# A recurrent-attention and mixture-of-experts kernel: two more blocks of the first expert ahead of the recurrence's end, conversions behind evictions, w2 after the tokens

## The chip, the cores and the metric

One core of one Trainium2 chip runs the whole kernel. The metric is the device time of one execution in microseconds (us). The engines are TensorE (PE, with its weight loads PEld), VectorE (DVE), ScalarE (ACT), GpSimd (POOL) and SyncE (SP), which here only issues DMAs.

## The reference

Two stages follow each other. The first is a linear recurrence over 768 steps for 4 x 8 heads of width 40; the second sends each of the 3072 rows to one of 8 experts.

```python
for t in range(S):                       # S = 768, state is [B, H, 40, 40]
    y[:, :, t] = einsum('bhd,bhde->bhe', rt, state)
    Sa = einsum('bhde,bhe->bhd', state, at)
    state = state * wt[:, :, None, :] - einsum('bhd,bhe->bhde', Sa, bt)
    state = state + einsum('bhd,bhe->bhde', vt, kt)
x = y.transpose(0, 2, 1, 3).reshape(3072, 320)

logits = x @ w_gate                      # 8 experts
e_idx = argmax(logits, axis=1)
gate_w = softmax(logits)[e_idx]
eom = sigmoid(x @ w_output_gate)
for e in range(8):                       # w1: 320 x 1024, w2: 1024 x 320
    h = maximum(x[e_idx == e] @ w1[e], 0)
    out[e_idx == e] = gate_w * eom[:, e] * (h @ w2[e])
```

## The kernel before

**The recurrence.** Time is cut into 12 chunks (c) of 64 steps. The heads of a chunk form two groups, q = 0 and 1; (11,1) is the last group of the recurrence. For each group `crit` carries the state on, and `tail` forms the output: transposes (ptS, ptU), products pM, a mask M on DVE, the sums pY on PE, and x = pY times the decays on DVE. `route` then works on x: it writes x to DRAM (xd), transposes it on PE (pxt from ident and x), copies the result to xT on ACT, and multiplies it by the gate weights (pxt from G and xT).

**The router.** `pick` runs four times, the last time for chunk 11. On DVE it finds the best expert of each row (a one-hot table in mem), PE counts rows with matmuls on two constant matrices (tri, one), and DVE turns the counts into a slot number si. POOL then scatters records into a table in DRAM (tab). `slots` reads the table back (tr), and DVE makes tb and ti of it: for each slot of each expert the row and its weight. An expert has 480 slots in 4 tiles of 120.

**Tokens.** `tokens` has POOL gather rows of xd by ti into xg (one indirect DMA a tile), transposes them on PE in three pieces k (px), and splits each into a rounded part xh (ACT) and a remainder xl (DVE); the third piece has two more copies on ACT. A product is the sum of three rounded products (high x high, high x low, low x high).

**Weights.** `weights` loads w1 in three pieces and w2 in three (st, by SP), casts each to its high part on ACT (w1h, w2h) and subtracts on DVE for the low part (w1l, w2l). Two sets of weight buffers are used in turn, and four staging buffers st.

**An expert.** `expert` has 8 blocks. In each, eight matmuls fill a PSUM tile ph; ACT evicts it as hh = relu, and DVE as hl, the remainder. In the experts' stage there are three buffers for ph. Then for each tile of tokens 24 matmuls (three for each block) fill po, DVE scales it to y, and POOL scatters y to the output. The first two experts are done in halves of two tiles (240 slots), because half of the table is known after chunk 7; experts 2 to 7 are done whole (480 slots).

**What is early.** `early` runs as background work inside the recurrence: it converts the first expert's weights, gathers the tokens of its first half, and computes the first E0 = 4 of its 8 blocks. There ph is a tile of the recurrence's PSUM pool (px_ and a number in the rows of the order). The other blocks run in `experts`, where `unit` steps through the blocks and tiles of one expert and lets a second generator, `prep`, go one step for each: next weights and next tokens.

**What sets the order.** The code gives dependencies and priorities, and a scheduler sets the order on each engine. Each engine then works through its own order and waits where data are not there. `issue_after` adds an order between two instructions. Before the change `s.last`, the end of the last pick, is what the conversions of the second expert's weights (st1) come after.

Of the kernel before, what the change touches and what calls it, by code (L numbers as in the profile page):

```python
# [9 lines left out]
F32 = mybir.dt.float32  # L10
# [4 lines left out]
AF = mybir.ActivationFunctionType  # L15
ALU = mybir.AluOpType
# [38 lines left out]
class Att:  # L55
# [441 lines left out]
    def run(s, sink, first, then, last):  # L497

        n = s.nch
        done = object()  # L500
        batches = [[c] for c in range(FAST)] + [list(range(c, min(c + 2, n))) for c in range(FAST, n, 2)]
        ready = {}

        def preps(b):
            for c in b:
                yield from s.prep(c)
                if c + 1 < n:
                    s.scan(c + 1)
                if c == 0:
                    with s.tc.issue_after(s.mark[1]):  # L510
                        s.later()

        def inv(b):
            yield from s.tinv(b)
            for c in b:
                ready[c] = True

        def background():
            s.warm(s.ident, 40)
            s.scan(0)  # L520
            for b in batches:
                yield from preps(b)
                if b == batches[0]:
                    first()
                yield from inv(b)
            s.pre.close()
            s.idle = True
            if then:
                yield from then()
        bg = background()  # L530
        npc = 0

        def adv(k):
            for _ in range(k):
                next(bg, done)

        def need(c):
            while c not in ready:
                next(bg)
        need(0)  # L540
        with s.tc.issue_after(s.mark[1]):
            s.load_r(0, 0)
            s.load_x(0, 0)
            s.load_x(0, 1)
        tail = iter(())

        def later(k):
            while k and s.post:
                if next(s.post[0], done) is done:
                    s.post.pop(0)  # L550
                else:
                    k -= 1
        for c in range(n):
            need(min(c + 1, n - 1))
            for q in range(2):
                for i, _ in enumerate(s.crit(c, q)):
                    next(tail, None)
                    if i == 3:
                        with s.tc.issue_after(s.mark['am', 1]):
                            if q == 0:  # L560
                                s.load_r(c, 1)
                            elif c + 1 < n:
                                s.load_r(c + 1, 0)
                            if c + 1 < n:
                                s.load_x(c + 1, q)
                    adv(RATE)
                    later(1)
                while next(tail, done) is not done:
                    pass
                tail = s.tail(c, q, sink)  # L570
        last()
        for _ in tail:
            pass
        later(-1)
        for _ in bg:
            pass


E, CAP, DM, FF, NTOK = 8, 480, 320, 1024, 3072
TS = CAP // 4  # L580
E0 = 4


class Moe:
# [48 lines left out]
                s.nc.sync.dma_start(out=s.G[d:128, k, 8 * j:8 * j + 8], in_=x[r:r + 128 - d])  # L633
        s.nc.sync.dma_start(out=s.tab.rearrange("(p n) f -> p n f", p=128), in_=s.t0)

    HALF, HT, half = 7, 2, False
    NB = {3: (0, 4), 7: (4, 4), 10: (8, 3), 11: (11, 1)}

    def route(s, c, q, x, pool, psx):

        nc = s.nc
        xf = x.rearrange("p h e -> p (h e)")
        nc.sync.dma_start(out=s.xd[256 * c + 128 * q:256 * c + 128 * q + 128], in_=xf)
        pt = psx()
        for k, o in enumerate((0, 128, 192)):
            nc.tensor.transpose(out=pt[:, k], in_=xf[:, o:o + 128], identity=s.ident)
        xT = pool.tile([128, 3, 128], F32, name="xT", tag="xT", bufs=1)
        nc.scalar.copy(out=xT, in_=pt[:, 0:3])
        for k in range(3):
            nc.tensor.matmul(pt[:, 3], xT[:, k], s.G[:, k], start=(k == 0), stop=(k == 2))  # L650
        nc.scalar.copy(out=s.LG[:, 2 * c + q], in_=pt[:, 3, 0:16])
        yield
        if q and c in s.NB:
            yield from s.pick(*s.NB[c], pool, psx().rearrange("p k t -> p (k t)"))
            if c == s.HALF:

                nc.vector.tensor_tensor(out=s.base, in0=s.base, in1=s.bnd, op=ALU.max)
                s.half = True

    def pick(s, c0, n, pool, fl):  # L660
# [31 lines left out]
        V.tensor_tensor(out=sv, in0=pr, in1=ro(s.base), op=ALU.add)  # L692
        pe = fl[:, 224:232]
        for i in range(n):
            nc.tensor.matmul(pe, s.one, oh[:, i], start=(i == 0), stop=(i == n - 1))
        V.tensor_tensor(out=s.base, in0=s.base, in1=pe, op=ALU.add)
        yield
        ov = wv
# [61 lines left out]
    def weights(s, e, wp, sp, lag=0, mark=None, st=()):  # L760
# [21 lines left out]
        if not lag:  # L782
            for k in range(6):
                with ExitStack() as order:
                    for m in s.last if st else ():
                        order.enter_context(s.tc.issue_after(m))
                    halve(k, st[k] if k < len(st) else load(k))
                yield
            return
# [41 lines left out]
    def expert(s, nt, W, T, pool, ps1, ps2):  # L831
# [5 lines left out]
        for f in range(8):  # L837
            fs = slice(128 * f, 128 * f + 128)
            ph = ps1()[:, 0:TS * nt]
            seq = []  # L840
            for k in range(2):
                seq += [(w1h[:, k, fs], xh[:, k]), (w1h[:, k, fs], xl[:, k]), (w1l[:, k, fs], xh[:, k])]
            seq += [(w1h[:, 2, fs], xh[:, 2]), (w1h[:, 2, fs], xl[:, 2])]
            for i, (l, r) in enumerate(seq):
                nc.tensor.matmul(ph, l, r, start=(i == 0), stop=(i == 7))  # L845
            p, w = pool()
            a = p.tile([128, w], F32R, name="hh", tag="hh")[:, 0:TS * nt]
            b = p.tile([128, w], F32R, name="hl", tag="hl")[:, 0:TS * nt]
            nc.scalar.activation(out=a, in_=ph, func=AF.Relu)  # L849
            nc.vector.scalar_tensor_tensor(out=b, in0=ph, scalar=0.0, in1=a.bitcast(F32), op0=ALU.max, op1=ALU.subtract)  # L850
            hh.append(a)
            hl.append(b)
            yield
# [24 lines left out]
    def early(s, ctx, psx, mark):  # L878
# [21 lines left out]
        s.hp0 = ExitStack()  # L900
        hp = s.hp0.enter_context(s.tc.tile_pool(name="hp0", bufs=E0, side="right"))
        s.hp = hp, TS * 2
        s.E0 = s.expert(2, s.W0, T, lambda: s.hp, lambda: s.ps1(), lambda: s.ps2())
        s.ps1 = lambda: psx(CAP)
        for _ in range(E0):
            next(s.E0)
            yield

    def experts(s, ctx, verdict):
        tc = s.tc  # L910
# [29 lines left out]
        tabs = s.slots(tp)  # L940
        t2 = tok(tabs, 0, 2, 2)
        unit(0, 0, 2, chain(t, w))
        s.hp0.close()
        t3 = tok(tabs, 1, 2, 2)
        unit(1, 0, 2, t2)
# [4 lines left out]
        for e in range(2, E):  # L950
            n = e + 1 < E
            t = tok(tabs, e + 1, 0, 4) if n else iter(())
            with ExitStack() as order:
                if not n:
                    order.enter_context(tc.manual_schedule(engines={mybir.EngineType.PE}))
                unit(e, 0, 4, chain(wts(e + 1), t) if n else t)


class General:
# [174 lines left out]
```

## Time and profile before

| | us |
|---|---|
| median of 3 runs | 692.04 |
| lowest and highest | 689.71 to 692.27 |
| profiled execution | 689.8 |
| span of its trace (first to last instruction) | 688.0 |
| mean granted clock of TensorE | 0.966 |

The span is cut into instructions of each engine. A row of the timeline has the start, the time, the engine, the line, the operation with its tiles, and in brackets the idle time ahead of it and what ended it. Matmuls overlap, so what one costs in a sequence is the distance between starts, not its own time. A granted clock of 1.00 is 2.4 GHz, one of 0.50 is 1.2 GHz.

### The profile page before, as it was taken

Reading aid. Unit: us, or ns where it says so; the run is one execution under the profiler, and the core shown is the slowest. Engines: PE = TensorE matmul, PEld = TensorE weight load, DVE = VectorE, ACT = ScalarE, POOL = GpSimd, SP = SyncE. Lnnn points to the kernel's source line nnn. Section 1 sums busy time; section 2 is a strip of 40 time slices with the busy share of each in tenths; the row PEclk is TensorE's granted clock in tenths of the full one; section 3 lists DMA queues with packets and bytes.
Section 4 is the critical chain, followed back from the end, with each engine's and each line's share of the span. In section 5 each row is a group of like instructions: output and inputs, shape, how many; then the busy total and the mean of one; then the engine's idle time right before and its main releaser. Section 6 shows DMA issues by size and latency. Waiting matters only on the chain.

```text
span 688.0 us, 21149 instructions
## 1 busy us (share of the span) xinstructions
PE 636.0 (92%) x8871; PEld 567.0 (82%) x8871; DVE 464.1 (67%) x911; ACT 339.7 (49%) x783; POOL 237.3 (34%) x337
## 2 busy tenths in 40 slices
PE   7687988898999999989999799799999999999995
PEld 6466877787888888888888798799999998898985
DVE  8868689969986995998499544453774455554230
ACT  2577752874477367537733434433562344333120
POOL 9665321341333458214223201445242152412112
PEclk9667999999999999999999899899999999999999
DMA  6995763376356537633225722352674343521001
GB/s 139 175 190 129 177 154 68 91 174 161 99 144 168 118 86 192 164 87 113 64 78 170 209 83 81 98 159 80 200 219 117 112 135 110 190 79 33 19 11 32
DMA packets 56305, 84.45 MB, mean 123 GB/s; under 512 B 26848, under 2 KB 43515, under 8 KB 54763
## 3 DMA queue, kind: packets, MB, share of 16 engines
q1 hardware_dynamic: 52331, 74.05, 41.5%
q0 software_dynamic: 3872, 8.97, 4.5%
q8 instruction: 72, 1.18, 0.7%
q14 instruction: 30, 0.25, 0.1%
HBM read 67.59 MB, written 8.96 MB: 111 GB/s over the span
## 4 chain that ended last, share of the span: by engine, by line
PE 55%; DVE 24%; ACT 8%; DMA 7%; issue 5%; SPq 1%; POOLq 0%; POOL 0%; ACTq 0%; DVEq 0%
PE ph L845 12%; PE pa L392 5%; PE po L860 4%; PE pM L464 4%; PE po L858 4%; PE po L859 4%; DVE tmpf L314 4%; PE pl L225 4%; PE pt L163 3%; ACT N L236 3%; DVE I L116 2%; PE pS L430 2%; DVE P L116 2%; DMA out_dram<-y,ti 2%; DMA st<-in_w_dram 2%
## 5 line engine op out<-in xcount | busy, mean ns | idle before, releaser
L850 DVE SCALAR_TENSOR_TENSOR hl<-ph,hh 128x480 fp32r<-128x480 f32 (+1 forms) x76 | 41.9, 562 | 62.3 <-ACT hh L849 58.2
L863 POOL DMA_INDIRECT out_dram<-y,ti x32 | 35.3, 1104 | 137.1 <-DVE y L862 73.6
L845 PE MATMUL ph<-xh,w1h 128*128 128x480 f32 (+1 forms) x228 | 79.7, 352 | 1.7 <-DVE hl L850 1.3
L849 ACT ACTIVATE hh<-ph 128x480 fp32r<-128x480 f32 (+1 forms) x76 | 37.0, 498 | 89.5 <-PE ph L845 84.9
L858 PE MATMUL po<-w2h,hh 128*120 128x320 f32 x256 | 78.9, 312 | 0.9 <-ACT hh L849 0.9
L845 PE MATMUL ph<-xl,w1h 128*128 128x480 f32 (+1 forms) x228 | 78.4, 346 | 0.0
L859 PE MATMUL po<-w2l,hh 128*120 128x320 f32 x256 | 77.9, 308 | 0.0
L860 PE MATMUL po<-w2h,hl 128*120 128x320 f32 x256 | 76.2, 310 | 0.0
L240 POOL TENSOR_SCALAR_AFFINE_SELECT LA<-LA 64x192 f32<-64x192 f32 x144 | 54.7, 413 | 42.2 <-ACT LA L238 40.8
L225 PE MATMUL pl<-Am,KBt 120*128 120x192 f32 (+1 forms) x288 | 60.9, 343 | 7.5 <-ACT LA L238 7.0
L383 ACT ACTIVATE As<-pa,hq 128x320 f32<-128x320 f32 x80 | 42.1, 528 | 47.5 <-PE pa L392 35.8
L236 ACT ACTIVATE N<-pl 32x192 f32<-32x192 f32 (+1 forms) x138 | 51.5, 374 | 25.8 <-PE pa L392 12.2
L726 POOL DMA_INDIRECT tab<-rec,si x24 | 29.0, 1209 | 89.8 <-DMA tab<-rec,si 37.2
L480 PE MATMUL pY<-KB,M 128*64 128x64 f32 (+1 forms) x768 | 53.5, 225 | 3.1 <-DVE M L468 3.0
L225 PEld LDWEIGHTS pl<-Am,KBt 120*128 120x128 f32 x288 | 45.3, 199 | 13.3 <-ACT LA L238 9.6
L464 PE MATMUL pM<-R,VU 128*128 128x128 f32 x384 | 52.9, 289 | 1.1 <-ACT VU L456 1.1
L479 PE MATMUL pY<-Sd,R 128*64 128x64 f32 (+1 forms) x704 | 54.0, 227 | 0.0
L392 PE MATMUL pa<-As,Tc 64*32 64x40 f32 x1792 | 51.1, 204 | 2.3 <-ACT As L383 1.7
L480 PEld LDWEIGHTS pY<-KB,M 128*64 128x64 f32 x768 | 47.0, 138 | 6.8 <-DVE M L468 3.4
L845 PE MATMUL ph<-xh,w1l 128*128 128x480 f32 (+1 forms) x152 | 52.5, 345 | 0.0
L814 POOL DMA_INDIRECT xg<-xd,ti x32 | 38.7, 1210 | 33.7 <-PE px L822 16.7
L392 PEld LDWEIGHTS pa<-As,Tc 64*32 64x32 f32 x1792 | 40.2, 112 | 12.1 <-issue 3.5
(198 smaller groups left out, 1574.0 us busy)
## 6 DMA issues: line engine op xcount, KB each, us to landing
D<-in_din_dram SPq DMA_DIRECT2D x12, 1080.0 KB
st<-in_w_dram SPq DMA_DIRECT2D x16, 512.0 KB
st<-in_w_dram SPq DMA_DIRECT2D x16, 480.0 KB
XS<-in_vt_dram SPq DMA_DIRECT2D x24, 256.0 KB
XU<-in_vt_dram SPq DMA_DIRECT2D x24, 256.0 KB
VU<-in_vl_dram SPq DMA_DIRECT2D x24, 208.0 KB
w<-in_win_dram SPq DMA_DIRECT2D x12, 371.2 KB
st<-in_w_dram SPq DMA_DIRECT2D x16, 256.0 KB
```

Of the source, the lines that this page charges most:

```text
L225: nc.tensor.matmul(pl[:, i, 0:nj], KBt[:, 6 * side + g0 + i].rearrange("p n t -> p (n t)"), Am[:, g0 + i:g0 + i + 6 * nj - 5:6, 0:64], sta ...
L236: s.mark['n', c] = nc.scalar.activation(out=nn, in_=pn, func=AF.Copy, scale=-1.0).ins
L240: g.affine_select(out=la[:, :, i], in_=la[:, :, i], pattern=[[0, nj], [1, C]], base=0, channel_multiplier=-1, compare_op=ALU.is_gt, fill=0.0)
L383: s.mark['as'] = nc.scalar.activation(out=x, in_=pa, func=AF.Copy, scale=s.hq[:, h:h + 1]).ins
L392: nc.tensor.matmul(pa[o + w:o + w + 32, i], m(p)[o:o + 64], x[o:o + 64, i, :], start=start, stop=True, tile_position=(o, o + w), skip_grou ...
L464: nc.tensor.matmul(pM[:, i], VU[:, h0 + i].rearrange("p n t -> p (n t)"), R[:, :, h0 + i], start=True, stop=True)
L479: nc.tensor.matmul(o, R[:, side, i, :], Sf[:, 40 * i:40 * i + w], start=True, stop=False)
L480: s.mark['y'] = nc.tensor.matmul(o, Ms[i // 4][:, i % 4, side, :], Kf[:, k:k + w], start=not c, stop=True).ins
L845: nc.tensor.matmul(ph, l, r, start=(i == 0), stop=(i == 7))
L858: nc.tensor.matmul(po, hh[f][:, ts_], w2h[:, f], start=(f == 0), stop=False)
L859: nc.tensor.matmul(po, hh[f][:, ts_], w2l[:, f], start=False, stop=False)
L860: nc.tensor.matmul(po, hl[f][:, ts_], w2h[:, f], start=False, stop=(f == 7))
```

## The change

Six blocks of the first expert run early in place of four. Blocks 4 and 5 are not left to the scheduler's own place: `pins` orders their matmuls behind marked instructions of the recurrence's end. Four matmuls of block 4 come after pY of group (11,0) (mark a), four after the transposes of x of (11,1) (mark d), and all eight of block 5 after the gate matmuls of (11,1) (mark e). Marks b, c and f are collected and not used. The conversion of the second expert's second w1 piece is ordered after the evictions of block 6, and that of all later pieces after those of block 7. For experts 2 to 6 the preparation of the next one has w1's three pieces first, then the tokens, then two empty steps, then w2's three pieces; before it was w1, w2, tokens.

```diff
         last()
+        s.mark['a'] = s.mark['y']
         for _ in tail:
             pass
         later(-1)
+        s.mark['c'] = s.mark['y']
+        s.mark['over'] = True
         for _ in bg:
             pass
...
-E0 = 4
+E0 = 6
...
             for k in range(6):
                 with ExitStack() as order:
-                    for m in s.last if st else ():
+                    for m in (*s.last, *s.wait.get({1: 6, 2: 7, 3: 7, 4: 7, 5: 7}.get(k), ())) if st else ():
                         order.enter_context(s.tc.issue_after(m))
...
             for i, (l, r) in enumerate(seq):
-                nc.tensor.matmul(ph, l, r, start=(i == 0), stop=(i == 7))
+                with s.tc.issue_after(s.pins[f, i]) if (f, i) in s.pins else ExitStack():
+                    nc.tensor.matmul(ph, l, r, start=(i == 0), stop=(i == 7))
...
+            if s.wait is not None:
+                s.wait[f] = hi, lo
...
+        s.wait = {}
         s.E0 = s.expert(2, s.W0, T, lambda: s.hp, lambda: s.ps1(), lambda: s.ps2())
         s.ps1 = lambda: psx(CAP)
-        for _ in range(E0):
+        for _ in range(4):
             next(s.E0)
             yield
+        while 'over' not in mark:
+            yield
+        at = dict(a=mark['a'], b=s.at['g', 11, 0], c=mark['c'], d=s.at['t', 11, 1], e=s.at['g', 11, 1], f=s.at['p'])
+        s.pins = {(4 + i // 8, i % 8): at[m] for i in range(8 * (E0 - 4)) for m in 'adee'[i // 4]}
+        for _ in range(4, E0):
+            next(s.E0)
+            yield
+        s.pins = {}
...
-                unit(e, 0, 4, chain(wts(e + 1), t) if n else t)
+                w = wts(e + 1) if n else t
+                unit(e, 0, 4, chain(islice(w, 3), t, iter("  "), w) if n else t)
```

**The end of the recurrence.** On PE, before, behind the sums pY of the last group: the transposes of x, the gate matmuls, and the matmuls of the last pick.

```order
L479 MATMUL pY<-Sd,R_152 64x40
L480 MATMUL pY<-KB,M 64x40
L646 MATMUL pxt<-ident,x 128x128 x3
L650 MATMUL pxt<-G,xT 128x128 x3
L687 LDWEIGHTS tri
L687 MATMUL pxt<-mem,tri 128x16
L689 LDWEIGHTS one
```

In the change, at the same place (px_6943 is block 4, px_6956 block 5; four more matmuls of block 5 follow, then tri).

```order
L480 MATMUL pY<-KB,M 64x40
L650 MATMUL pxt<-ident,x 128x128 x3
L850 MATMUL px_6943<-xl,w1h 128x240
L850 MATMUL px_6943<-xh,w1l 128x240
L850 MATMUL px_6943<-xh,w1h 128x240
L850 MATMUL px_6943<-xl,w1h 128x240
L654 MATMUL pxt<-G,xT 128x128 x3
L850 MATMUL px_6956<-xh,w1h 128x240
L850 MATMUL px_6956<-xl,w1h 128x240
L850 MATMUL px_6956<-xh,w1l 128x240
L850 MATMUL px_6956<-xh,w1h 128x240
```

The second half of block 4 and all of block 5 have moved in front of the last pick; the first half of block 4 stands, in the same way, between pY and the transposes of x of group (11,0). On DVE, before, the last pick ran through the one-hot table and the slot count without a break:

```order
L682 TENSOR_REDUCE mem<-mem 128x2
L719 TENSOR_REDUCE mem<-mem 128x2
L684 TENSOR_TENSOR mem<-mem 128x2x8
L720 TENSOR_SCALAR mem<-mem 128x2
L692 TENSOR_TENSOR mem<-pxt,base 128x2x8
```

In the change, with the line numbers moved by four:

```order
L686 TENSOR_REDUCE mem<-mem 128x2
L723 TENSOR_REDUCE mem<-mem 128x2
L688 TENSOR_TENSOR mem<-mem 128x2x8
L855 SCALAR_TENSOR_TENSOR hl<-px_6956,hh 128x240
L724 TENSOR_SCALAR mem<-mem 128x2
L696 TENSOR_TENSOR mem<-pxt,base 128x2x8
```

The eviction hl of block 5 now stands between the one-hot table and the slot count.

**The first transposes of tokens gathered by the whole table.** On PE, before: the end of the second expert's first three blocks (ph), the transposes px, and the first po of that expert.

```order
L845 MATMUL ph<-xh,w1h 128x240 x3
L845 MATMUL ph<-xl,w1h 128x240 x3
L845 MATMUL ph<-xh,w1l 128x240
L845 MATMUL ph<-xh,w1h 128x240
L845 MATMUL ph<-xl,w1h 128x240
L822 MATMUL px<-ident,xg 128x120 x4
L858 MATMUL po<-w2h,hh 120x320
```

In the change, at the same transposes:

```order
L850 MATMUL ph<-xh,w1l 128x240
L850 MATMUL ph<-xh,w1h 128x240
L850 MATMUL ph<-xl,w1h 128x240
L865 MATMUL po<-w2h,hh 120x320
L826 MATMUL px<-ident,xg 128x120 x2
L866 MATMUL po<-w2l,hh 120x320
L850 MATMUL ph<-xh,w1h 128x240
```

Three more blocks of the second expert (24 ph) and 12 of its po now stand ahead of these transposes; the 48 po of the first expert's first half stand ahead of them in both.

**From one whole expert to the next.** On ACT, before (hh are evictions, the w1h and w2h casts are the next expert's weights, xh and xl its tokens):

```order
L849 ACTIVATE hh<-ph 128x480 x5
L774 CAST w1h<-st 128x1024 x3
L824 CAST xh<-px 64x480
L827 CAST xh<-px 64x480
L828 CAST xl<-xl 64x480
L779 CAST w2h<-st 128x960 x2
L779 CAST w2h<-st 128x640
L849 ACTIVATE hh<-ph 128x480 x3
```

In the change:

```order
L828 CAST xh<-px 64x480
L831 CAST xh<-px 64x480
L832 CAST xl<-xl 64x480
L854 ACTIVATE hh<-ph 128x480 x2
L778 CAST w1h<-st 128x1024 x3
L854 ACTIVATE hh<-ph 128x480
L783 CAST w2h<-st 128x960 x2
L783 CAST w2h<-st 128x640
L854 ACTIVATE hh<-ph 128x480 x3
```

The tokens' third piece has moved ahead of the w1h casts, and one eviction hh has moved between the w1h and the w2h casts.

## Rows read from the trace of the kernel before

**Rows 1.** The page's first part: busy us, share of the span, instructions.

```profile
PE 636.0 (92%) x8871; PEld 567.0 (82%) x8871; DVE 464.1 (67%) x911; ACT 339.7 (49%) x783; POOL 237.3 (34%) x337
```

**Rows 2.** Timeline of PE around the recurrence's end.

```profile
429.41 0.55 PE L646 MATMUL pxt<-ident,x 128*128 128x128 f32 x3 [1.24 <-DVE x L482]
...
436.80 0.55 PE L646 MATMUL pxt<-ident,x 128*128 128x128 f32 x3 [0.58 <-DVE x L482]
437.96 0.94 PE L650 MATMUL pxt<-G,xT 128*128 128x128 f32 x6 [0.62 <-ACT xT L648]
440.21 0.20 PE L687 MATMUL pxt<-mem,tri 128*128 128x16 bf16 x1 [1.31 <-DVE mem L684]
...
441.23 0.54 PE L845 MATMUL ph<-xh,w1h 128*128 128x240 f32 x1 [0.34 <-DVE mem L700]
...
443.06 0.60 PE L822 MATMUL px<-ident,xg 120*128 120x120 f32 x2
...
458.95 0.73 PE L822 MATMUL px<-ident,xg 120*128 120x120 f32 x4 [1.23 <-DMA xg<-xd,ti]
```

**Rows 3.** Windows of 1 us: PE, PEld, DVE, ACT, POOL busy, clock, DMA share, GB/s.

```profile
439.00:440.00 1.00, 0.00 (x0) 0.00 (x0) 0.76 (x6) 0.33 (x2) 0.69 (x2) 0.63 0.00 0
...
446.00:447.00 1.00, 1.00 (x9) 1.00 (x9) 0.97 (x2) 1.00 (x4) 0.00 (x0) 0.95 0.79 226
```

**Rows 4.** The chain that ended last: start, us, what.

```profile
460.26 0.90 PE ph L845 x8
...
557.46 3.27 PE ph L845 x15
560.74 0.15 PE po L858
...
564.10 0.16 PE po L860
```

**Rows 5.** Timeline of DVE and ACT at the last pick and the second expert's weights.

```profile
440.46 0.17 DVE L692 TENSOR_TENSOR mem<-pxt,base 128x16 f32<-128x16 f32 x1 [0.23 <-PE pxt L689]
...
448.46 0.40 DVE L850 SCALAR_TENSOR_TENSOR hl<-ph,hh 128x240 fp32r<-128x240 f32 x1
...
442.66 2.94 ACT L774 CAST w1h<-st 128x1024 fp32r<-128x1024 f32 x3 [0.73 <-DVE si L709]
...
446.40 0.36 ACT L849 ACTIVATE hh<-ph 128x240 fp32r<-128x240 f32 x1
```

**Rows 6.** Timeline of POOL and DVE between the pick and the gathers.

```profile
448.78 1.00 POOL L726 DMA_INDIRECT tab<-rec,si  x1 [5.04 <-DMA st<-in_w_dram]
454.41 1.13 POOL L814 DMA_INDIRECT xg<-xd,ti  x1 [4.63 <-DVE xl L825]
...
453.42 0.27 DVE L873 COPY tb<-tr 120x128 f32<-120x128 f32 x1 [1.50 <-DMA tr<-tab]
...
453.93 0.18 DVE L875 CAST ti<-tb 120x64 int32<-120x64 f32 x1
```

**Rows 7.** Waits of PE from 460 on: us in total, times, longest.

```profile
PE ph L845 <- DVE hl L850: 1.3, 3, 0.4
PE po L858 <- ACT hh L849: 0.9, 3, 0.3
```

**Rows 8.** Timeline of ACT, DVE and PE at one transition between whole experts.

```profile
564.28 2.52 ACT L779 CAST w2h<-st 128x960 fp32r<-128x960 f32 x3 [7.09 <-PE po L860]
566.71 1.49 ACT L849 ACTIVATE hh<-ph 128x480 fp32r<-128x480 f32 x3
...
568.19 1.78 DVE L850 SCALAR_TENSOR_TENSOR hl<-ph,hh 128x480 fp32r<-128x480 f32 x3
...
566.05 0.98 PE L822 MATMUL px<-ident,xg 120*128 120x120 f32 x8
567.32 0.41 PE L858 MATMUL po<-w2h,hh 128*120 128x320 f32 x1 [0.29 <-ACT hh L849]
...
568.90 0.48 PE L845 MATMUL ph<-xh,w1h 128*128 128x480 f32 x1 [0.43 <-DVE hl L850]
```

More of the change, by code (lines that the diff above doesn't have):

```diff
@@ L634, in loads @@
         s.nc.sync.dma_start(out=s.tab.rearrange("(p n) f -> p n f", p=128), in_=s.t0)
-    HALF, HT, half = 7, 2, False
+    HALF, HT, half, wait = 7, 2, False, None
+    at, pins = {}, {}
     NB = {3: (0, 4), 7: (4, 4), 10: (8, 3), 11: (11, 1)}
@@ L645, in route @@
         for k, o in enumerate((0, 128, 192)):
-            nc.tensor.transpose(out=pt[:, k], in_=xf[:, o:o + 128], identity=s.ident)
+            s.at['t', c, q] = nc.tensor.transpose(out=pt[:, k], in_=xf[:, o:o + 128], identity=s.ident).ins
         xT = pool.tile([128, 3, 128], F32, name="xT", tag="xT", bufs=1)
@@ L649, in route @@
         for k in range(3):
-            nc.tensor.matmul(pt[:, 3], xT[:, k], s.G[:, k], start=(k == 0), stop=(k == 2))
+            s.at['g', c, q] = nc.tensor.matmul(pt[:, 3], xT[:, k], s.G[:, k], start=(k == 0), stop=(k == 2)).ins
         nc.scalar.copy(out=s.LG[:, 2 * c + q], in_=pt[:, 3, 0:16])
@@ L694, in pick @@
         for i in range(n):
-            nc.tensor.matmul(pe, s.one, oh[:, i], start=(i == 0), stop=(i == n - 1))
+            s.at['p'] = nc.tensor.matmul(pe, s.one, oh[:, i], start=(i == 0), stop=(i == n - 1)).ins
         V.tensor_tensor(out=s.base, in0=s.base, in1=pe, op=ALU.add)
@@ L848, in expert @@
             b = p.tile([128, w], F32R, name="hl", tag="hl")[:, 0:TS * nt]
-            nc.scalar.activation(out=a, in_=ph, func=AF.Relu)
-            nc.vector.scalar_tensor_tensor(out=b, in0=ph, scalar=0.0, in1=a.bitcast(F32), op0=ALU.max, op1=ALU.subtract)
+            hi = nc.scalar.activation(out=a, in_=ph, func=AF.Relu).ins
+            lo = nc.vector.scalar_tensor_tensor(out=b, in0=ph, scalar=0.0, in1=a.bitcast(F32), op0=ALU.max, op1=ALU.subtract).ins
+            if s.wait is not None:
+                s.wait[f] = hi, lo
             hh.append(a)
@@ L942, in experts @@
         unit(0, 0, 2, chain(t, w))
+        s.wait = None
         s.hp0.close()
```

## The prediction

> **What bounds the kernel now.** I read the page first, then the waits of TensorE (PE) in the second half, then PE's timeline around the end of the recurrence, the granted clock there, and last the queues behind the waits that I found. PE is busy 92% of the span [rows 1], so what is left to win is short stretches in which it waits or runs at half clock. There are two kinds of place.
>
> The first is the last 30 us of the recurrence and the start of the experts [rows 2]. PE waits 1.24 us for x of group (11,0), 0.58 us for x of (11,1), 0.62 us for xT, 1.31 us for the one-hot table of the router's last pick, 0.34 us before the first block in the expert stage (ph), and 1.23 us at the transposes of gathered tokens (px, 458.95). That is 5.3 us of idle. The clock is lost too: PE does nothing in 439:440, the granted clock falls there (0.63 in the mean of that stretch) and is back in 446:447 [rows 3]. Block 4 takes from 441.23 to 443.06, 1.83 us [rows 2], where a block at full clock takes 0.90 [rows 4].
>
> The wait at 458.95 is the end of another chain: the pick gives the slots, scatters write the table (the last at 448.78), a read brings it back, tb and ti are made (453.42, 453.93), and two gathers are issued (the first at 454.41), whose data PE waits for [rows 6]. So this moment is set by DMA, not by PE: whatever PE gains or loses before it goes into that wait, and a gain counts only as work that is done before the wait and no longer after it.
>
> The second kind is the transition from one expert to the next. From 460 on, PE waits 1.3 us for hl and 0.9 us for hh, three times each, nothing else [rows 7]. In the one at 567 the three casts of w2h hold ScalarE (ACT) from 564.28 for 2.52 us, the three evictions of the new expert's first blocks come behind them at 566.71, and PE waits 0.29 us and 0.43 us [rows 8]: 0.72 us each.
>
> **The change part by part.** *Blocks 4 and 5 ahead of the experts.* The order shows four matmuls of block 4 behind pY of (11,0), four behind the transposes of (11,1), and block 5 behind the gate matmuls. A block is eight matmuls in 0.90 us [rows 4], so these are 0.45, 0.45 and 0.90 us in waits of 1.24, 0.62 and 1.31 us [rows 2]. Each fits, so they cost nothing; without these covers they would cost their 1.8 us. Their evictions use ACT 0.36 us and VectorE (DVE) 0.40 us each [rows 5]. Block 4's are over before DVE's pick begins. Block 5's hl stands in DVE's order between the one-hot table and L692, which ran at 440.46 [rows 5]. Block 5 starts near 438.8 and ends near 439.8; with 0.36 us of ACT and 0.40 of DVE behind it L692 starts near 440.7. So the pick, the scatters queued behind it and the first ph are 0.2 us later.
>
> A rule speaks against this order. The row first: block 4 was through PE at 443.06, yet its hh ran at 446.40, behind casts that began at 442.66 [rows 2, 5]. The page "TensorE: Matmul & The Clock Gate" of the Trainium skill (Part 1, Architectural detail) calls the queues of ScalarE and VectorE strictly first in, first out; the trace agrees, and by that rule a late block 5 delays the whole pick. With block 5 at half clock the sum would hold 0.9 us more in place of 0.2.
>
> *Conversions behind evictions.* Before, hh of blocks 4 and 5 stood behind the casts of the second expert's weights. Now the second cast of w1 waits for block 6, the rest for block 7. Nothing is added: it is a new order on ACT and DVE. PE reaches the second expert's blocks later in its program, after all 48 po: from 441.4, two blocks (1.8), three pairs of transposes (0.3 each, half of the 0.60 at half clock in [rows 2]) and 48 po (7.1; 24 took 3.52 us, 0.147 each [rows 4]) end at 451.2. ACT's casts take 2.94 us for w1 and 2.52 for w2 [rows 5, 8]; begun near 443.1, with two evictions and the token copies between, they are through near 450, and DVE follows piece by piece. Only the last xl comes behind that, and it is needed some 2.3 us into the new blocks. I cost this at nothing; if that cover goes, xl's lateness is PE's.
>
> *What stands ahead of the DMA-bound wait.* Before it, the program now holds 24 more ph and 12 more po. By [rows 4] that is 24 x 0.112 + 12 x 0.147 = 2.7 + 1.8 = 4.4 us of work that no longer lies after it. PE gets there at 451.2 + 48 x 0.112 + 12 x 0.147 = 458.3, plus about 0.3 for evictions, still before 458.95. The data: 0.2 us later by the pick, 0.3 us earlier because ti now follows tb directly (0.51 us apart before [rows 6], with an hl between). One thing is added in that chain: on GpSimd's queue (POOL) an output scatter now stands ahead of the gathers. Its y is ready near 452, and the gathers cannot start before 454, so the scatter's 1.1 us hide; late, they would cost 1.1 us and 0.3 of issue. Bounds for the moment of the wait: 0.3 us earlier to 1.4 later. I take 0.2 later. Gain here: 4.4 - 0.2 = 4.2 us, bounds 3.0 to 4.7.
>
> *w2 late.* For experts 2 to 7 the weights' first three pieces come first, then tokens, then w2. On ACT the order now puts one hh ahead of the w2h casts, on PE eleven ph, 24 po and 21 ph where 15, 24 and 9 stood. The first block is thus evicted during the 24 po (3.5 us), and between the start of the casts and the first po that reads the new blocks lie 21 ph of 0.218 us [rows 4] and 8 transposes of under 1.0 in all, some 5.4 us. In [rows 8] the third hh ends 3.9 us after the first cast and the third hl 5.7 us after it; the first is in time, and the last has nine po (1.3 us) more before it is read. So I take all three waits as gone: 3 x 0.72 = 2.2 us [rows 7], bounds 0 and 2.2; I book 2.1.
>
> **The sum.** 4.2 + 2.1 = 6.3 us. The profiled execution took 689.8 us on a span of 688.0; it becomes 683.5. The three timed runs lie at 689.71, 692.04 and 692.27, so the profiled one is near the lowest; the median less 6.3 is 685.7. Two of four runs lie low and two high, so I forecast in between, nearer the median: 685.0.
>
> **Rivals.** *The clock falls all the same.* Waits that stay, 439.8 to 440.2 and 440.5 to 441.4, could bring it to half. Then blocks 6 and 7 take 1.83 us each and some po are slow; with a half-clock stretch as long as the one in [rows 3] PE comes to the gathers 2.2 us later, near 460.4, and the first gain shrinks to 4.4 - 1.4 = 3.0. Time 686.3. For it: gaps stay. Against it: with 1.35 us more work between 437 and 440, PE is busier there than in [rows 3]. The same page of the Trainium skill (Part 1, What you observe) holds that the moment of a transition varies from run to run with an unchanged program; no single trace here can show that.
>
> *The w2 waits stay.* If evictions still collide with the casts, only 4.2 is gained: 687.1. For it: three casts and three hh keep their order. Against it: the block ahead of them.
>
> *Little of it happens.* The clock falls and the w2 waits stay: 3.0 us, 688.5; or the table's chain slips by 2 to 3 us with the w2 waits staying, 690. Under no change at all 691 to 692.
>
> *Slower.* DVE now makes both y of expert 0 ahead of tb. The second y needs the last of the 48 po. Should that po end after the table's read lands (453.4), tb, ti and the gathers are late by the same amount, one for one, and the longer wait at px can bring the half clock back for some 2.4 us more. It turns into a loss beyond 6.3 us, that is, with the last po after 457.3 with the clock falling, 459.7 without. Against it: the po would have to be over 6 us later than worked out.
>
> **Chances.** Forecast 0.55, clock falling 0.15, w2 waits staying 0.12, little 0.13, slower 0.05. A difference under 0.5% (3.5 us) cannot be told from none with this kernel: below 688.6 is faster, above 695.5 slower. The first two cases and most of the third, and part of the fourth, are faster: 0.78. Same 0.18, slower 0.04. The range reaches from 682, the lowest run less 6.3 with the upper bound of 4.7 and a run's scatter, to 690, where the cases with little gain lie.
>
> **What would show it.** Right: px_ blocks 4 and 5 inside the old waits; granted clock 1.00 through 438 to 446; a wait of 0.5 to 1 us for xg at about 459, with the second expert's block 5 behind PE; no wait for hh or hl between 560 and 640; the span near 681.7. Wrong: hl of block 5 holding L692 beyond 440.9; the output scatter or y holding the gathers beyond 455; a new wait at the fourth block of an expert, or at the first po behind the transposes.

## The result, and the profile after

| | us |
|---|---|
| before, median of 5 runs | 691.09 (689.71 to 692.27) |
| after, median of 5 runs | 685.20 (678.93 to 687.68) |
| ratio | 0.9885, 95% interval 0.9835 to 0.9934 |
| profiled execution after | 687.68, span 685.9, the slowest of the five |

The change is faster by 1.15%, 685.2 us against 685.0 forecast. That the two agree so well is luck: the profiles show that two errors of the forecast met in this number. Three slow executions (3145.31 us in e4, 701.65 in e8, 699.61 in e10) count in the medians and ranges below, but not in the ratios.

PE's busy time, beside [rows 1]:

```profile
PE 633.7 (92%) x8871; PEld 566.5 (83%) x8871; DVE 465.5 (68%) x911; ACT 339.3 (49%) x783; POOL 228.0 (33%) x337
```

Timeline of PE around the recurrence's end, after; it answers to [rows 2]. The px rows with w1h are the pinned blocks.

```profile
432.06 0.38 PE L850 MATMUL px<-xh,w1h 128*128 128x240 f32 x1
...
439.89 0.55 PE L650 MATMUL pxt<-ident,x 128*128 128x128 f32 x3 [0.58 <-DVE x L482]
440.19 0.36 PE L850 MATMUL px<-xl,w1h 128*128 128x240 f32 x1
...
441.06 0.94 PE L654 MATMUL pxt<-G,xT 128*128 128x128 f32 x6 [0.18 <-ACT xT L652]
441.75 0.36 PE L850 MATMUL px<-xh,w1h 128*128 128x240 f32 x1
...
443.30 0.18 PE L691 MATMUL pxt<-mem,tri 128*128 128x16 bf16 x1 [0.40 <-DVE mem L686]
...
444.49 0.35 PE L850 MATMUL ph<-xh,w1h 128*128 128x240 f32 x1 [0.34 <-DVE base L700]
...
446.81 0.29 PE L826 MATMUL px<-ident,xg 120*128 120x120 f32 x1 [1.20 <-DMA xg<-xd,ti]
448.62 0.32 PE L826 MATMUL px<-ident,xg 120*128 120x120 f32 x1 [1.51 <-DMA xg<-xd,ti]
...
466.36 0.37 PE L826 MATMUL px<-ident,xg 120*128 120x120 f32 x2
```

Blocks 4 and 5 stand in the old waits: the wait for xT fell from 0.62 to 0.18, that for the one-hot table from 1.31 to 0.40. Block 6 follows at 444.49. Then PE waits 1.20 and 1.51 us for xg, at the tokens of the second expert's first half. This profile of the kernel before had no wait there. At 466.36, the transposes of tokens gathered by the whole table, there is no wait, where before had 1.23. The clock, in windows of 1 us with the columns of [rows 3]:

```profile
447.00:448.00 1.00, 0.10 (x1) 0.00 (x0) 0.00 (x0) 0.00 (x0) 0.36 (x1) 1.00 0.82 262
448.00:449.00 1.00, 0.38 (x3) 0.39 (x4) 0.00 (x0) 0.00 (x0) 0.00 (x0) 0.94 1.01 347
449.00:450.00 1.00, 1.00 (x7) 1.00 (x7) 0.41 (x1) 0.97 (x2) 0.00 (x0) 0.50 1.08 299
```

It stayed at 1.00 through the recurrence's end, and fell after PE had done little in 447 and 448. POOL and DVE between the pick and the gathers, after, answering to [rows 5] and [rows 6]:

```profile
443.73 0.17 DVE L696 TENSOR_TENSOR mem<-pxt,base 128x16 f32<-128x16 f32 x1
...
458.88 0.55 DVE L869 TENSOR_SCALAR y<-po,tb 120x320 f32<-120x320 f32 x1 [0.32 <-PE po L867]
459.35 0.27 DVE L880 COPY tb<-tr 120x128 f32<-120x128 f32 x1
459.65 0.20 DVE L882 CAST ti<-tb 120x64 int32<-120x64 f32 x1
...
443.47 1.14 POOL L818 DMA_INDIRECT xg<-xd,ti  x1 [0.30 <-issue]
444.91 1.11 POOL L818 DMA_INDIRECT xg<-xd,ti  x1 [0.31 <-issue]
...
459.45 1.09 POOL L870 DMA_INDIRECT out_dram<-y,ti  x1 [5.35 <-DVE y L869]
460.85 1.13 POOL L818 DMA_INDIRECT xg<-xd,ti  x1 [0.30 <-issue]
```

The two gathers that PE waited for issued at 443.47 and 444.91, behind six table scatters on POOL's queue. The waits of PE from 455 on, answering to [rows 7]:

```profile
PE po L865 <- ACT hh L854: 0.2, 1, 0.2
```

Timeline of ACT at the transition of [rows 8]:

```profile
562.01 0.57 ACT L854 ACTIVATE hh<-ph 128x480 fp32r<-128x480 f32 x1 [5.67 <-PE ph L850]
566.09 2.52 ACT L783 CAST w2h<-st 128x960 fp32r<-128x960 f32 x3 [3.51 <-PE po L867]
568.51 1.04 ACT L854 ACTIVATE hh<-ph 128x480 fp32r<-128x480 f32 x2
```

One eviction stands ahead of the casts and two behind; PE waits for none of the three.

**A yardstick.** x of (11,1) came at 436.25 us before and at 439.35 after, though the order up to there is the same but for the pinned blocks; over all profiles of this study it lies between 432.61 and 443.44. So I compare stretches instead of ends: from x (DVE, L482) to the start of the last po on PE. It has two parts: to the first px by the whole table (458.95 before, 466.36 after), and from there to the last po. Each is a difference of two starts in the timeline.

| profiled execution | first-half gather, after x | px by the whole table, after x | px to last po | stretch |
|---|---|---|---|---|
| before | 2.0 | 22.7 | 221.3 | 244.02 |
| before, second profile (e2) | 4.0 | 24.4 | 221.6 | 245.95 |
| after | 4.1 | 27.0 | 212.7 | 239.67 |
| after, second profile (e1) | 2.0 | 22.7 | 212.8 | 235.51 |
| after, third profile (e9) | 4.7 | 29.4 | 212.4 | 241.84 |
| w2 late alone (e3) | 2.0 | 22.2 | 217.7 | 239.96 |
| all but w2 late (e4) | 1.7 | 22.5 | 216.5 | 238.99 |
| gathers early (e5) | 34.1 ahead of x | 22.9 | 212.6 | 235.47 |
| no eviction order (e6) | 2.0 | 22.9 | 213.3 | 236.11 |
| four blocks (e7) | 2.0 | 24.3 | 218.9 | 243.18 |
| spare blocks (e8) | 2.0 | 21.6 | 220.8 | 242.42 |
| gathers held (e10) | 5.5 | 30.2 | 212.4 | 242.54 |
| gathers early, again (e11) | 32.3 ahead of x | 23.0 | 212.5 | 235.50 |

The last part can be cut once more, at the first block of the third expert, which is the first ph of 480 columns. Timeline of PE before, then after:

```profile
500.88 0.38 PE L845 MATMUL ph<-xh,w1h 128*128 128x480 f32 x1
...
680.27 0.30 PE L860 MATMUL po<-w2h,hl 128*120 128x320 f32 x1
```

```profile
503.62 0.38 PE L850 MATMUL ph<-xh,w1h 128*128 128x480 f32 x1
...
679.02 0.31 PE L867 MATMUL po<-w2h,hl 128*120 128x320 f32 x1
```

From the first px by the whole table to this block PE took 41.9 us before and 37.3 after. From this block to the last po it took 179.2 to 179.5 us in the four profiles with the old order of w2 (before, e2, e4, e8) and 175.4 to 175.5 in the nine with the new one.

### The profile page after: what moved, and what is told of

The parts are those of the page before. It is cut to its first block, busy times and chain, and to the rows that moved or that the text cites. A ratio compares the mean times of both kernels' runs of the same rounds, so it can differ in the third digit from the quotient of the medians.

```text
span 685.9 us, 21154 instructions
## 1 busy us (share of the span) xinstructions
PE 633.7 (92%) x8871; PEld 566.5 (83%) x8871; DVE 465.5 (68%) x911; ACT 339.3 (49%) x783; POOL 228.0 (33%) x337
## 5 line engine op out<-in xcount | busy, mean ns | idle before, releaser
L870 POOL DMA_INDIRECT out_dram<-y,ti x32 | 33.7, 1054 | 141.3 <-DVE y L869 87.0
L850 PE MATMUL ph<-xh,w1h 128*128 128x480 f32 (+1 forms) x222 | 76.6, 349 | 0.3 <-DVE base L700 0.3
L850 PE MATMUL ph<-xl,w1h 128*128 128x480 f32 (+1 forms) x222 | 76.1, 346 | 0.0
L225 PE MATMUL pl<-Am,KBt 120*128 120x192 f32 (+1 forms) x288 | 62.7, 351 | 8.6 <-ACT LA L238 6.6
L225 PEld LDWEIGHTS pl<-Am,KBt 120*128 120x128 f32 x288 | 47.0, 205 | 14.2 <-ACT LA L238 9.0
L392 PEld LDWEIGHTS pa<-As,Tc 64*32 64x32 f32 x1792 | 40.2, 112 | 14.7 <-ACT As L383 5.2
L850 PE MATMUL ph<-xh,w1l 128*128 128x480 f32 (+1 forms) x148 | 51.0, 345 | 0.0
L464 PEld LDWEIGHTS pM<-R,VU 128*128 128x128 f32 x384 | 46.5, 195 | 2.7 <-ACT VU L456 1.2
```

What stands on the lines that cost most here:

```text
L225: nc.tensor.matmul(pl[:, i, 0:nj], KBt[:, 6 * side + g0 + i].rearrange("p n t -> p (n t)"), Am[:, g0 + i:g0 + i + 6 * nj - 5:6, 0:64], sta ...
L392: nc.tensor.matmul(pa[o + w:o + w + 32, i], m(p)[o:o + 64], x[o:o + 64, i, :], start=start, stop=True, tile_position=(o, o + w), skip_grou ...
L464: nc.tensor.matmul(pM[:, i], VU[:, h0 + i].rearrange("p n t -> p (n t)"), R[:, :, h0 + i], start=True, stop=True)
```

## The experiments

Theory: the gain is moved work plus a cleaner transition, and the first profile lost part of it to late gathers. Rivals: the clock is what is gained; the late chain behind the table, not the first-half gathers, is what is lost; the eviction order carries part of the gain.

**The two kernels again.** e1 is the change and e2 the kernel before, both unedited.

> The changed kernel once more, unedited, for a second profile. In its first profile TensorE waits 1.2 and 1.5 us for the gathered tokens of the second expert's first half (px behind block 6), and the clock falls behind that wait. Theory A: these gathers stand behind six table scatters on GpSimd, so the wait is part of the change and comes again, 2 to 3 us, and the time is near 685. Theory B: the scatters were slow by chance in that execution; then the wait is under 1 us, the first part of the change gives its 4.2 us, and the profiled execution is near 682.

> The kernel before once more, unedited, for a second profile, to see how far two executions of one program differ up to the end of the recurrence. Theory A: the 3.1 us by which the changed kernel's recurrence ended later are such a difference; two profiles of the kernel before differ there by 1 to 3 us as well, while the stretch from x of (11,1) to TensorE's end takes 244.0 us again, within 1. Theory B: the 3.1 us belong to the change; then this profile has x of (11,1) at 436 as the first one.

e1: 679.09 us median of 6, ratio 0.9824 (0.9794 to 0.9854); e2: one execution, 692.79. In e1's timeline the gathers are early, and the same places read:

```profile
440.67 0.97 POOL L730 DMA_INDIRECT tab<-rec,si  x1 [1.42 <-DVE x L482]
441.94 1.14 POOL L818 DMA_INDIRECT xg<-xd,ti  x1 [0.30 <-issue]
...
446.49 0.32 PE L826 MATMUL px<-ident,xg 120*128 120x120 f32 x1 [0.15 <-DMA xg<-xd,ti]
...
462.63 0.37 PE L826 MATMUL px<-ident,xg 120*128 120x120 f32 x2
```

x was at 439.96, so these are 2.0, 6.5 and 22.7 us after it. The wait is down to 0.15, the clock stays at 1.00, and the stretch is 4.2 us shorter than in the first profile of the same kernel. The kernel before has the same two kinds of execution: in e2 the gathers came 4.0 us after x, and PE waited 2.0 us for them, but that cost it only 1.9 us of stretch.

So e1's wait is as its Theory B has it, though its profiled execution took 684.83 us and not 682: x came 3.7 us later in it than in the first profile of the kernel before. For e2 neither theory holds as written: x came 0.8 us later than in the first profile, but the stretch is 1.9 longer. That the 3.1 us are not the change's is shown by e9, where the changed kernel has x at 432.61.

**Each gain alone.** e3 is the kernel before with the last hunk of the diff; e4 is the change without it.

```diff
 e3, on before; e4 has the - line on the change
-                unit(e, 0, 4, chain(wts(e + 1), t) if n else t)
+                w = wts(e + 1) if n else t
+                unit(e, 0, 4, chain(islice(w, 3), t, iter("  "), w) if n else t)
```

> The kernel before with nothing but the order w1, tokens, w2 for experts 2 to 6. The prediction's 2.1 us: 689.0 against 691.1, a ratio of 0.997. Theory A, from the starts of matmuls: each of the three transitions loses 1.25 us from start to start (0.72 of it shown as idle), so 3.7 us: 687.4, ratio 0.9946, and the stretch from x of (11,1) to TensorE's end falls from 244.0 to 240.3. Nothing gained: 691.

> The change without its last edit: six blocks early and conversions behind evictions, with w1, w2, tokens as before. The prediction's 4.2 us: 686.9, ratio 0.994, stretch from x of (11,1) to TensorE's end 239.8. Theory A, by which the wait for the second expert's tokens eats most of it: 0.4 to 1.5 us, 690, ratio 0.998 to 0.999, stretch near 243, with waits of some 2.7 us at px behind block 6. The three waits of 0.72 us between experts stay in both.

e3: 686.69, ratio 0.9934 (0.9907 to 0.9960), beside a before of 690.94. e4: 688.06, ratio 0.9950 (0.9921 to 0.9978). In the stretches w2 late is worth 244.02 - 239.96 = 4.1 us and the rest 244.02 - 238.99 = 5.0. Cut at the third expert, w2 late gives 179.4 - 175.4 = 4.0 behind it, and the rest 41.9 - 37.2 = 4.8 (rounded from 41.93 and 37.17) ahead of it. The medians do not add up like this: against 690.94 they are 4.3 and 2.9 us lower singly, and 11.9 together (e1), more than the stretches give. They include the part ahead of x, and the causes are read from the stretches here, not from them. Theory A of e4 falls in its profile: the gathers came 1.7 us after x and PE had no wait for them. e4's waits of PE from 450 on keep the three transitions:

```profile
PE ph L850 <- DVE hl L855: 1.3, 3, 0.4
PE po L865 <- ACT hh L854: 1.1, 4, 0.3
```

**The gathers' place.** e5 lets the background work of the recurrence issue the two first-half gathers, so that POOL has them ahead of the eight scatters.

```diff
-        m = 2 if pool is s.tp0 else 4
+        m = 2 if pool in (s.tp0, s.tp1) else 4
...
+        s.tp1 = pool("tp1", 1)
+        s.t10 = s.tokens(s.tabs, 1, 0, 2, s.tp1, lambda n: s.psx(n))
+        s.T10 = next(s.t10)
+        next(s.t10)
...
-        t = tok(s.tabs, 1, 0, 2)
+        s.psx = psx
+        t, T[1, 0] = s.t10, s.T10
```

> The change, but the two gathers of the second expert's first-half tokens are issued from the background work of the recurrence, so that on GpSimd's queue they stand ahead of the eight table scatters of the last pick instead of behind six of them. PE, DVE and ACT keep their order. Theory A (where these gathers come late, PE's wait for them and the half clock behind it are a loss of the change, as in its first profile): no wait of PE for xg between 440 and 455, no granted clock of 0.50 there, and a stretch from DVE's x of group (11,1) to PE's last po of 235 to 236 us whatever the scatters do; the median at or up to 1.5 us below that of the change (679.1 in the session before), and the highest run below 684. Theory B (the gathers' place is of no account, the late executions come from elsewhere): the stretch still takes both 235.5 and 239.7 in executions, and the times spread as before. Theory C: the gathers ahead of the scatters hold the table back by the 2 us that they take to issue on GpSimd, so PE waits at the first transposes of tokens gathered by the whole table (none is shown in the undisturbed profile of the change): stretch 237.5, median about 681.

e5: 684.61 (681.43 to 688.26), ratio 0.9880 (0.9844 to 0.9915). Stretch 235.5, as Theory A had it, but the scatters were early in this profile, so it could not tell the theories apart; the median, on another chip, is not below that of e1 as a ratio, and the highest run is 688.26, where Theory A wanted less than 684. Theory C falls: px by the whole table came 22.9 us after x, and the stretch is not 237.5. The question is taken up by e9 to e11.

**No eviction order.** e6 drops the waits of the conversions on blocks 6 and 7.

```diff
-                    for m in (*s.last, *s.wait.get({1: 6, 2: 7, 3: 7, 4: 7, 5: 7}.get(k), ())) if st else ():
+                    for m in (*s.last, *()) if st else ():
```

> The change without its order of the second expert's weight conversions behind the evictions of blocks 6 and 7. The prediction booked that order at nothing. Theory A: it is worth nothing, 679 (685 in an execution with the late gathers). Theory B: the order is what keeps the evictions of blocks 6 and 7 ahead of the casts; without it PE waits for hh in the first expert's po, 1 to 2 us more, and reaches the gathers later: 680 to 681.

e6: 684.60, ratio 0.9894 (0.9850 to 0.9938). The stretch is 0.6 us longer than e1's, which the times cannot resolve, and PE waits for hh in the first po no longer than in e1 (0.2 us in both). By this one pair of profiles the order is worth 0.6 us, near the nothing at which I booked it.

**Four blocks.** e7 is the change with `E0 = 4`.

> The change with four early blocks in place of six: no block of the first expert is pinned to the end of the recurrence; eviction order and w2 behind the tokens stay. Theory A (the first gain is the work of the two blocks in waits of PE, the second the w2 order): only the second is left, 3.7 to 4.0 us on a kernel before of 691, so 687.2, as with w2 late alone (686.7 in the session before), and the granted clock falls near x of (11,1) + 3 us as in the kernel before. Theory B (the eviction order brings part of the first gain): 685 or less.

e7: 689.66, ratio 0.9953 (0.9927 to 0.9980), no better than w2 late alone: Theory A in the times, and Theory B falls. The clock fell too, to 0.50 by 445 to 446, some 6 us after x. The profile is worse than A expected, since a wait has appeared:

```profile
463.56 0.39 PE L826 MATMUL px<-ident,xg 120*128 120x120 f32 x2 [3.53 <-DMA xg<-xd,ti]
...
458.50 1.11 SPq L750 DMA_DIRECT2D st<-in_w_dram  x2
```

As I read it, later conversions free the staging buffers later: the next weights' loads start at 458.50, 0.8 us after the first gather by the whole table (457.71), where in e1 they start 2.9 us before it. So without the pinned blocks the eviction order seems to cost in this execution; one profile does not show it, nor how often it would.

**Spare blocks.** e8 is the kernel before with 16 matmuls, copies of those of blocks 4 and 5 with unused results, at the pinned places. It does more work than the kernel before, and blocks 4 and 5 still come late.

```diff
...
+            for i, (l, r) in enumerate(seq):
+                with s.tc.issue_after(at['adee'[2 * j + i // 4]]):
+                    s.nc.tensor.matmul(ph, l, r, start=(i == 0), stop=(i == 7))
...
```

> The kernel before with 16 more matmuls, copies of those of blocks 4 and 5 whose results nothing uses, in the places of the pinned blocks; blocks 4 and 5 themselves are done later, as before. It separates the work moved from the clock kept. Theory A (the gain is work that no longer lies behind the wait for the gathers): the granted clock stays at 1.00 past x of (11,1), PE reaches the transposes px of (0,2) earlier, and the wait there grows by as much; time as before, 690 to 691.5. Theory B (the clock is what the change gains): the fall of 440 to 447 is gone and the time is 2.4 us lower, 688.5.

e8: 691.40, ratio 0.9975 (0.9944 to 1.0006). The clock is kept. From 4.9 to 5.9 us after x the window reads as follows; the second one is of the kernel before at nearly the same distance, 4.75 to 5.75:

```profile
443.00:444.00 1.00, 0.94 (x8) 0.98 (x9) 0.96 (x12) 0.21 (x1) 0.00 (x0) 1.00 0.56 149
```

```profile
441.00:442.00 1.00, 0.77 (x4) 0.80 (x4) 0.96 (x12) 0.21 (x1) 0.00 (x0) 0.50 0.39 108
```

The times can tell this neither from no gain nor from the 2.4 us of Theory B, whose ratio of 0.9965 lies in the interval. The stretch decides. It is 1.6 us shorter; 1.1 of that are an earlier px (21.6), where the table's read was issued 0.7 us sooner, and that a full clock did this was not tried apart. From px to the third expert's first block PE took 41.6 us, 0.3 less than before, and here PE had four more po (0.6 us) ahead of px than before. In e4, which has the clock and the moved work, it took 37.2. So a kept clock alone does not give the 4.8 us, and the rival "the clock is the gain" fails as the whole of it. With the moved work in place PE reaches px about when its data do, and a lost clock would count there; e8 does not price that.

**Held and early gathers, side by side.** e9 is the change once more; e10 puts an idle POOL operation ahead of the two gathers; e11 is e5 again. All three ran on one chip.

```diff
 e10
...
+        if (e, t0) == (1, 0):
+            with s.tc.issue_after(s.at['s', 8]):
+                nc.gpsimd.affine_select(out=xg.rearrange('p m d -> p (m d)')[:, 0:960], in_=s.W0[0][0:TS, 0, 0:960].bitcast(F32),
+                                        pattern=[[1, 960]], compare_op=ALU.is_ge, fill=0.0, base=0, channel_multiplier=0)
```

> The change once more, as the reference for the two kernels that run beside it. A stretch from x of (11,1) to the last po of 235.5 us where the first-half gathers issue 2.0 us after x, of 239.7 where they issue 4.1 us after it; the median 0.983 to 0.989 of the kernel before.

> The change with one idle operation on GpSimd (960 columns, about 2.1 us by the 433 ns that 192 columns take in the trace) between the sixth table scatter and the two gathers of the second expert's first-half tokens, so that these issue about 4.1 us after x of (11,1) in every execution, as they did by themselves in the first profile of the change. The order on PE, DVE and ACT is that of the change. Theory A (late gathers alone make the loss of that profile): PE waits for xg twice, some 1.2 and 1.5 us, the granted clock falls behind them, the transposes px of (0,2) start 26 to 27 us after x of (11,1) in place of 22.7, stretch 239 to 240; the median 3 to 4 us above that of the change. Theory B (late gathers are only a sign of the late scatter chain, which is what costs): the chain is early here, so PE waits 2.7 us less later on, px of (0,2) stays near 23 to 24, stretch 235.5 to 237; the median within 1 us of the change.

> The change with the two gathers ahead of all eight table scatters, again, now beside the change itself. Theory A (only executions with late gathers gain): no wait for xg between 440 and 455, stretch 235 to 236, the median equal to that of the change or up to 2 us lower. Theory B (nothing gained): the same median within 1 us, and a wait at px of (0,2) that is as long as the change's. If the scatter chain is late in this profile (the first scatter less than 12.3 us ahead of x of (11,1)), Theory A expects no wait at the first-half px and px of (0,2) near 24.5, by the kernel before's second profile (24.35).

| | median | lowest to highest | ratio |
|---|---|---|---|
| before | 693.93 | 690.70 to 698.19 | |
| e9, change | 685.65 | 683.10 to 691.67 | 0.9885 (0.9844 to 0.9927) |
| e10, held | 687.37 | 686.43 to 699.61 | 0.9900 (0.9867 to 0.9933) |
| e11, early | 681.55 | 679.16 to 684.75 | 0.9821 (0.9786 to 0.9855) |

The scatters were late in all three profiles: the first issued 11.6 us ahead of x, where e1 had 13.0. e9 and e11 differ by the gathers' place alone in the code. PE's rows in e9:

```profile
440.56 0.29 PE L826 MATMUL px<-ident,xg 120*128 120x120 f32 x1 [1.68 <-DMA xg<-xd,ti]
443.39 0.46 PE L826 MATMUL px<-ident,xg 120*128 120x120 f32 x1 [2.54 <-DMA xg<-xd,ti]
...
462.06 0.37 PE L826 MATMUL px<-ident,xg 120*128 120x120 f32 x2
```

One window of its clock, behind the second wait:

```profile
444.00:445.00 1.00, 1.00 (x7) 1.00 (x7) 0.41 (x1) 1.00 (x2) 0.00 (x0) 0.50 0.99 383
```

And in e11, with x at 440.20:

```profile
446.32 0.37 PE L826 MATMUL px<-ident,xg 120*128 120x120 f32 x2
...
463.21 0.40 PE L826 MATMUL px<-ident,xg 120*128 120x120 f32 x2 [0.57 <-DMA xg<-xd,ti]
```

e9 waits 4.2 us, and its clock is at half in the windows from 443 to 448; e11 waits only at the second place, 0.57. The stretches are 241.8 and 235.5, the medians 4.1 us apart. e9's gathers issued 4.7 us after x, and its stretch is 2.2 us above the 239.7 expected for 4.1. So late scatters with early gathers cost nothing that the stretch shows, as Theory A has it, though px by the whole table came 23.0 us after x and not 24.5.

The rival is the chain behind the table. In e9 PE had no wait at px by the whole table (462.06), so the chain did not hold it there; tb ran 22.5 us after x, behind the second y in DVE's order, and that y had waited 0.32 us for its po. The table's read had been issued at 17.1; in e1 tb ran 1.7 us after that issue. So tb and the gathers behind it were late because PE was. One thing these runs do not part: with the gathers out of the way the last scatter also issued earlier, 11.8 us after x in e11 against 14.7 in e9. How long PE would wait at the second place if the first waits were gone and the last scatter stayed at 14.7 is not shown.

In e10 the gathers came 0.9 us later after x than in e9, and the stretch is 0.7 us longer; its median is 1.7 us above that of e9, where 3 to 4 were expected, but e9 had late gathers by itself. The pick was late too, since a DVE operation took as long as the idle one (last section), so e10 says little by itself.

## Why the prediction came out as it did

**First gain: booked 4.2, measured 5.0 where the gathers are early (e4).** Its parts held. The pinned blocks cost PE nothing; L692 (now L696) came 4.21 us after x before and 4.38 after, so 0.17 later where 0.2 was booked; the clock stayed up. From px to the first block of the third expert PE needed 41.9 us before and 37.2 in e4: 4.8 us less, where 4.4 of moved work was worked out. PE came to px by the whole table 22.7 us after x (e1), where 22.4 was worked out. The wait of 0.5 to 1 us that was to stay there did not: PE shows none in the first profile, e1, e4 and e9, and 0.5 to 0.6 us in e5 and e11.

**What failed is the step "PE gets there at 451.2 + 48 x 0.112 + 12 x 0.147 = 458.3".** It counts the transposes of the second expert's first-half tokens by their durations and gives their data no due time. Before, a half-clock block (1.83 us) stood ahead of them; now it is one of 0.9, and PE is there 6.1 us after x in place of 6.8. With the gathers 4.1 us after x it waits 2.7 us (the kernel before 2.0, in e2), the clock falls, and all of it counts, since PE now reaches the next place just as its data do; the kernel before had 1.23 us of waiting there to absorb a part. The loss is 239.67 - 235.51 = 4.2 us, 6.3 in e9; before loses 1.9. Of the 4.2, 2.7 are the two waits; the half clock behind them shows in the same profile as 1.69 us for a block (448.70 to 450.39) in place of 0.90. I had named a half clock as a rival, at the pick's waits, where it did not happen.

**Second gain: booked 2.1, measured 4.0 to 4.1 (e3).** The mechanism was right: no wait for hh or hl between 560 and 640. The term 3 x 0.72 was mis-sized, because the idle time of a row starts at the modelled end of the matmul ahead of it. Timeline of PE in the kernel before, beside [rows 8]:

```profile
567.32 0.41 PE L858 MATMUL po<-w2h,hh 128*120 128x320 f32 x1 [0.29 <-ACT hh L849]
567.56 0.31 PE L859 MATMUL po<-w2l,hh 128*120 128x320 f32 x1
...
568.01 0.31 PE L858 MATMUL po<-w2h,hh 128*120 128x320 f32 x1
568.15 0.31 PE L859 MATMUL po<-w2l,hh 128*120 128x320 f32 x1
568.90 0.48 PE L845 MATMUL ph<-xh,w1h 128*128 128x480 f32 x1 [0.43 <-DVE hl L850]
569.22 0.38 PE L845 MATMUL ph<-xl,w1h 128*128 128x480 f32 x1
```

A po takes 0.146 from start to start, but 0.75 pass from 568.15 to 568.90: 0.60 lost, where 0.43 is shown. The matmul behind the wait then takes 0.32 in place of 0.218, 0.10 more. At the wait for hh it is 0.45 + 0.10: the eight transposes of [rows 8] start 0.103 us apart, so the last starts at 566.77 and po 0.55 us behind it, and the next po follows 0.24 us later in place of 0.146. So a transition loses 1.25 us, and three 3.75; 4.0 were measured. The Trainium skill's page "Perfetto Trace Analysis" (Per-engine timelines, Tensor Engine Instruction) says that TensorE's end times are estimated, not observed; these rows agree.

**The sum.** With early gathers 5.0 + 4.1 = 9.1 singly and 244.02 - 235.51 = 8.5 together, where 6.3 was booked; with late ones 244.02 - 239.67 = 4.4 in the first profile. The 9.1 holds some scatter of the part up to px: cut at the third expert the two are 4.8 + 4.0. The forecast of 685.0 lies between an under-sized gain and a loss that was not priced; that the median fell on it is luck.

**The other rivals.** The slower one's mechanism did occur: the second y (458.88) waited for its po and held tb, which ran 20.0 us after x, against 16.8 in e1. The first gather by the whole table issued 21.5 us after x there, beyond the 455 that was named as a sign of being wrong (18.75 after x). It cost no PE wait, since PE was later still. The w2 waits did not stay.

**Open.** Why the scatters are sometimes late. Relative to x the last pick but one came about 1 us later in such executions (si 12.2 to 12.5 us ahead of x, not 13.2 to 13.6), and single scatters issued up to 1.3 us further apart; it happened in 5 of 13 profiles, with either kernel.

## What to carry to other kernels

When work moves ahead of a wait for data, give every transfer between its new and its old place a due time: the moved work may have been the cover of one that never showed a wait. Issue a gather whose indices are known early ahead of unrelated scatters on the same queue; here that is worth 4.2 to 6.3 us of stretch in executions where the scatters run late. In the medians it is open: beside the change it was 681.55 against 685.65 (e11, e9), but the ratios to the kernel before, 0.9880 and 0.9821, are no better than the change's own 0.9885, 0.9824 and 0.9885. Price a TensorE wait from start to start, and compare stretches between two anchors when the part ahead of the change varies more than the change is worth.

## What the hardware showed that I had not expected

The recurrence's end varied by 11 us between executions of nearly one order (432.61 to 443.44), more than the change gains.

A GpSimd operation seems to have held DVE. In e10 a tensor-tensor operation on two SBUF operands, 0.17 to 0.18 us in the other twelve profiles, took 1.54 and ended as the idle operation on POOL did:

```profile
438.22 1.54 DVE L688 TENSOR_TENSOR mem<-mem 128x16 bf16<-128x16 f32 x1
...
438.72 1.00 POOL L819 TENSOR_SCALAR_AFFINE_SELECT xg<-w1h 120x960 f32<-120x960 f32 x1
```

The Trainium skill's page "SBUF — State Buffer" (SBUF: two separate sides) describes the port pair that these two engines share as an exclusive lock, also for a DVE operation with two SBUF inputs against a GpSimd operation that reads SBUF: the later one is blocked until the earlier ends. The two ends, 439.76 and 439.72, agree; POOL's start is too rough to read an order from.

A gather whose data move beside the weights' loads lands later. In e1 the second first-half gather issued at 443.39, and its data ended PE's wait 3.1 us later, as the loads were issued (446.50). In e9 the loads were issued at 439.16, 0.5 us after the second gather, and its data ended PE's wait 4.7 us after its issue. The view of DMA issues gives 3.9 us from issue to landing as the median of e9's two (the last column):

```profile
xg<-xd,ti POOLq DMA_INDIRECT x2, 3.9
```

In the window from 441 to 442 DMA moved 417 GB/s there (columns of [rows 3]):

```profile
441.00:442.00 1.00, 0.00 (x0) 0.00 (x0) 0.00 (x0) 0.00 (x0) 0.14 (x1) 1.00 1.12 417
```
